# A RetNet and MLP kernel: the first tiles' loads, the late decay tables and the planner's figures

## The chip, the cores and the metric

The kernel runs on one core of a Trainium2 chip. The metric is the device time of one execution in microseconds (us). The engines are PE (matrix products), DVE (vector), ACT (scalar activations), POOL (general purpose) and SP (which here only issues transfers). [...]

## The reference

```python
# q, k, v: (8, 8, 576, 64); x: (4608, 512); w_in: (512, 2048); w_out: (2048, 512); alpha: (2048,)
gamma = 1.0 - 2.0 ** (-5.0 - np.arange(H))
rel = pos[:, None] - pos[None, :]
Dmat = np.where(rel >= 0, gamma[:, None, None] ** rel, 0.0)
ret = (scale * np.matmul(q, k.T) * Dmat) @ v        # per batch and head
x = ret.transpose(0, 2, 1, 3).reshape(B * S, H * D)
h = x @ w_in
out = (np.maximum(h, 0) + alpha * np.minimum(h, 0)) @ w_out
```

First comes a retention layer (attention without softmax, weighted by a decay that falls with distance), then a two-layer MLP whose activation has a slope of its own for each hidden column. All of it is in 32 bit floats.

## The kernel before, in words

**Retention.** A batch has 576 rows, handled in chunks of 64. Within a chunk scores are masked and applied to v; across chunks a state per head is carried on. The decay is put into tables: `tp` holds factors for the rows of q and v, and `gch`, `tabx` and `tabk` hold factors for the carried state, for q and for k of the later pairs. All are computed by small DVE instructions at the head of the program (L117 to L157), before the planned part begins.

The first two batches are done in parts of 256, 256 and 64 rows (`load_part`, `part_scale`, `part_transposes`, `part_scores`, `part_states`, `part_carry`, `part_values`, `last_part`), all eight heads at a time. A part of 256 rows has two tiles each of k, q and v, of 128 rows by 512 columns (256 KB), numbered by `i` (0 is k, 1 is q, 2 is v) and `m`. POOL scales q and v by `tp` (L424); PE turns k and q with transposes (L448), which ACT copies out (L454); PE forms scores (L472), DVE masks them (L478), PE forms states (L494), DVE sums them (L506, L508), and PE forms values (L541, L557), which ACT copies into x (L572). `part_carry` (L514) decays the state for the next part. The other batches are done in pairs of heads (`joint`, with `operands` at L781 and L792), spread over the later work.

**MLP.** Tokens are taken in 18 blocks of 256. The first eight units of the first two blocks are multiplied as plain 32 bit floats (`unit_plain` L1039, `second_plain` L1070). All later ones split x, the weights and the activations into three pieces, and multiply these (`unit` L1108, `unit_two` L1138, `second` L1189). Weights are first converted (`convert`: ACT L670 and L672, DVE L680, L682 and L691, POOL L694) and then split (`split_w`, L723 to L735). The slopes come in as `a16`, 16 rows of 128, and are turned by one PE transpose (L1262) into `malpha` (L1264), which DVE reads for each activation.

**Order.** Nothing of this is issued as written. Each step is recorded by `do(engine, cost, function, reads, writes)`, and `plan()` draws one order: a backward pass gives each step a due time, and a forward pass picks for each engine, from the steps whose inputs would be there, the one that can start earliest, and among those within a small slack the one due first. The planner's clock starts for each engine at `BEGIN`, when the head of the program is taken to be over. A transfer costs 0.56 us of its issuing engine and then occupies one shared wire for its size over a rate; who reads it waits 2.0 us more. Of transfers planned within the first 100 us, an issue by SP also waits, on the chip, for an older one, so that at most 1.25 MiB are in flight (`IN_FLIGHT`, L220 is the line that issues). Steps with `lock` are kept from running beside a locked step of the other one of DVE and POOL.

The costs, the rates and `BEGIN` therefore don't only describe: a change of a figure can change the order of instructions on every engine, and with it which buffer is awaited when.

Of the kernel before, what the change touches and what calls it, by code (L numbers as in the profile page):

```python
# [21 lines left out]
def kernel(  # L22
# [55 lines left out]
    def half(x):  # L78
        return slice(x * C, (x + 1) * C)
# [15 lines left out]
    a16 = const.tile([NFC, P], FP32, name="a16")  # L95
    nc.scalar.dma_start(a16, moe_alpha.rearrange("(t p) -> t p", p=P))
    malpha = const.tile([P, NFC], FP32, name="malpha")
# [44 lines left out]

    nc.vector.reciprocal(pf[:, 1], pf[:, 1])
    nc.vector.tensor_tensor(out=th[:, 1], in0=pf[:, 1], in1=th[:, 2], op=ALU.mult)

    gch = const.tile([P, 3, NPAIR], FP32, name="gch")
    tabx = const.tile([P, NPAIR, 2], FP32, name="tabx")
    tabk = const.tile([P, NPAIR], FP32, name="tabk")
    for h2 in range(2):
        hd = slice(h2 * D, (h2 + 1) * D)  # L150
        nc.vector.tensor_copy(tabk[half(1 - h2)], th[half(1 - h2), 1, h2:H:2])
        nc.vector.tensor_copy(gch[hd, 0], th[hd, 2, h2:H:2])
        nc.vector.tensor_scalar(tabx[hd, :, 0], pf[hd, 0, h2:H:2], QSCALE, None, ALU.mult)
        nc.vector.scalar_tensor_tensor(out=tabx[hd, :, 1], in0=dif[hd, 5, h2:H:2], scalar=1.0,
                                       in1=tabx[hd, :, 0], op0=ALU.add, op1=ALU.mult)
    for i in range(2):
        nc.vector.tensor_tensor(out=gch[:, i + 1], in0=gch[:, i], in1=gch[:, i], op=ALU.mult)  # L157

    for i in range(2):
# [55 lines left out]

    RATE, RATE_256, RATE_128 = 236e3, 175e3, 115e3

# [124 lines left out]
    SLACK, SWITCH = {"PE": 0.3}, {"PE": 0.1}  # L342
    BEGIN = {"PE": 5.0, "ACT": 0.5, "DVE": 8.2, "POOL": 5.8, "SP": 0.5}

# [26 lines left out]
    w32m = [Gen(None) for _ in range(4 * NU)]  # L371
    cst = Gen(None)


# [31 lines left out]

    def load_part(x, which=(0, 1, 2)):
        j0, j1 = PARTS[x % 3]
        for i in which:
            for m in range((j1 - j0 + 1) // 2):  # L410
                s0 = (j0 + 2 * m) * C
                rows = min(P, j1 * C - s0)
                dma(lambda i=i, m=m, rows=rows: part(x, i)[0:rows, m],
                    lambda i=i, s0=s0, rows=rows: (k, q, v)[i][x // 3, :, s0:s0 + rows].rearrange(
                        "h p d -> p h d"), rows * DM * 4, (), [key_p(x, i, m)],
                    "ACT" if x == 0 and i == 1 else "SP", RATE_256)

# [18 lines left out]
    def part_transposes(x, i, bank):  # L436
        t = ((room[x, 3] if i == 0 else Gen((gs[0], op_)[x // 3])) if x % 3 == 0 else
             room[x + i, 3 - 2 * i])

        def at():  # L440
            return words_of(t)[:, 0:1024].rearrange("p (c s) -> p c s", c=NPAIR)
        tT[x, i] = t, at
        for m in range(2):
            pt = Gen(next(bank))

            def f(m=m, pt=pt):
                for c in range(NPAIR):
                    nc.tensor.transpose(pt.get()[:, c * P:(c + 1) * P],  # L448
                                        part(x, i)[:, m, 2 * c:2 * c + 2].rearrange(
                                            "p h d -> p (h d)"), ident)  # L450
            do("PE", 1.0, f, [key_p(x, i, m)], [(pt, 0)])

            def g(m=m, pt=pt):
                nc.scalar.copy(at()[:, :, m * P:(m + 1) * P],  # L454
                               pt.get().rearrange("p (c s) -> p c s", c=NPAIR))
            do("ACT", 0.59, g, [(pt, 0)], [(t, "t", m)])

    def part_scores(x, bank):
        a = Gen((gs[1], ats)[x // 3]) if x % 3 == 0 else room[x + 1, 2]

        def at():
            return words_of(a)[:, 0:1024].rearrange("p (h n) -> p h n", h=2)
        tat[x] = a, at
        (kt, kT), (qt, qT) = tT[x, 0], tT[x, 1]
        ps = [Gen(next(bank)) for _ in range(2)]
        for m in range(2):
            def f(m=m):
                for c in range(NPAIR):
                    for p2 in range(2):
                        for h2 in range(2):  # L470
                            j = chunk(2 * m + p2)
                            nc.tensor.matmul(  # L472
                                ps[h2].get()[half(p2), (2 * c + m) * C:(2 * c + m + 1) * C],
                                kT()[half(h2), c, j], qT()[half(h2), c, j], start=True, stop=True)
            do("PE", 0.9, f, [(kt, "t", m), (qt, "t", m)], [(ps[0], m), (ps[1], m)])
        for h2 in range(2):
            def g(h2=h2):
                nc.vector.tensor_tensor(  # L478
                    out=at()[:, h2].rearrange("p (n s) -> p n s", s=C),
                    in0=ps[h2].get().rearrange("p (n s) -> p n s", s=C),  # L480
                    in1=mask[:, None, :].to_broadcast([P, 8, C]), op=ALU.mult)
            do("DVE", 0.69, g, [(ps[h2], 0), (ps[h2], 1)], [(a, "m", h2)])
# [30 lines left out]
    def part_carry(x):  # L513
        do("POOL", 0.6, lambda: nc.gpsimd.tensor_tensor(  # L514
            out=carry_of(x + 1), in0=sums_of(x, 3),
            in1=gch[:, 2, :, None].to_broadcast([P, NPAIR, D]), op=ALU.mult),
            [sums_key(x, 3)], [carry_key(x + 1)], lock=True)

# [8 lines left out]
    def part_values(x, bank):  # L527
# [7 lines left out]
        for m in range(2):  # L535
            def f(m=m):
                for c in range(NPAIR):
                    for p2 in range(2):
                        for h2 in range(2):
# [5 lines left out]
                                             skip_group_check=True)  # L545
            do("PE", 0.7, f, [key_p(x, 2, m), (a, "m", 0), (a, "m", 1)], [(pv[0], 0), (pv[1], 0)])
        for m in range(2):
            js = [j for j in (2 * m, 2 * m + 1) if j or x % 3]

            def f(js=js):  # L550
                for j in js:
                    su = sums_of(x, j - 1) if j else carry_of(x)
                    for c in range(NPAIR):
                        for h2 in range(2):
                            for e in range(0, D, 32):
# [4 lines left out]
                                                 stop=(j >= 2), skip_group_check=True)  # L560
            do("PE", 0.8, f, [(qt, "t", m)] + [
                sums_key(x, j - 1) if j else carry_key(x) for j in js], [(pv[0], 0), (pv[1], 0)])
# [212 lines left out]
    def operands(n):  # L775
# [3 lines left out]
        def f():  # L779
# [3 lines left out]
                op=ALU.mult)  # L783
        do("POOL", 1.15, f, (), [(qx, a) for a in range(4)], lock=True)
        kT, qT = turned[n] = Gen(kTs[n % 2]), Gen(qTs[n % 2])
# [4 lines left out]
        def f():  # L790
            t = kn.get().rearrange("p j d -> p (j d)")
            nc.scalar.activation(t, t, ACTF.Copy, scale=tabk[:, c:c + 1])  # L792
        do("ACT", 0.78, f, (), [(kn, 0), (kn, 1)])

# [333 lines left out]
    def unit_two(va, vb, u, ga, f):  # L1128
# [3 lines left out]
        def mm():  # L1132
            for p, l in ((p0, 0), (p1, 2), (p0, 1)):
                for cc in range(NCC):
# [4 lines left out]
                                     start=(l != 1 and cc == 0), stop=(l > 0 and cc == NCC - 1))  # L1139
        do("PE", 2.755, mm, x_keys(va, 0) + x_keys(vb, 1) +  # L1140
           [w_at[u, i][l] for i in range(2) for l in range(3)], [(p0, 0), (p1, 0)], kind="pieces")
# [104 lines left out]
    for x in range(3):  # L1246
        rooms(x)
    load_part(0)
    bank = banks_of(0)
# [5 lines left out]
    weights(3)  # L1255
    part_states(0, bank)
    part_carry(0)
    part_values(0, bank)
    weights(1)
    fetch_x(visits[0])  # L1260
    aps = Gen(psa[0])
    do("PE", 0.2, lambda: nc.tensor.transpose(aps.get()[:, 0:NFC], a16, ident[0:NFC, 0:NFC]), (),  # L1262
       [(aps, 0)])
# [263 lines left out]
```

## Time and profile before

| | us |
|---|---|
| three runs, median (lowest to highest) | 943.56 (942.02 to 946.17) |
| the profiled execution, its own time | 940.2 |
| its span, first to last instruction | 938.5 |
| PE busy in the span | 915.6 |
| DVE, ACT, POOL busy | 532.7, 552.9, 578.2 |
| mean granted PE clock | 0.998 of full speed |
| read from HBM, written to it | 74.19 MB, 31.98 MB |

Busy times of different engines lie beside each other and don't add up. A matmul's end is modelled in the profile, so a busy PE is not one at its peak. "L448" is a line of the kernel before; in wait lists the engine or transfer after the arrow is the one that was seen to end last.

### The profile page before, as it was taken

The page shows a single profiled execution, that of the slowest core. Times are in us where ns is not written, and L with a number is a line of the kernel's source. Part 1 is how long each engine was busy: PE and PEld are TensorE (multiplying, and loading weights), DVE is VectorE, ACT ScalarE, POOL GpSimd, SP SyncE. Part 2 cuts the span into 40 slices and gives each one's busy share as a digit, 9 for nine tenths or more (in the row PEclk, how much of TensorE's full clock was granted, in tenths as well). Part 3 has the DMA queues.
Part 4 walks back from the last instruction along what each step waited for, and adds up shares of the span by engine and source line. Part 5 has one row for each costly group of instructions (what it writes and reads, how often), then busy time and mean ns, then how long its engine had stood idle before and what let it go on. Part 6 is the DMA issues. An engine that isn't in the chain of part 4 may idle for free.

```text
span 938.5 us, 21278 instructions
## 1 busy us (share of the span) xinstructions
PE 915.6 (98%) x8241; PEld 777.7 (83%) x8241; DVE 532.7 (57%) x1070; ACT 552.9 (59%) x1175; POOL 578.2 (62%) x491
## 2 busy tenths in 40 slices
PE   5898999999999999999999999999999999999998
PEld 4666688888889898888899988888888888888887
DVE  6668666575766766757664765443444444434333
ACT  4456566657767666665785875645546463635342
POOL 3657775738767577564676465748374656557363
PEclk9999999999999999999999999999999999999999
DMA  9967587788877778886425321121212122221112
GB/s 225 220 186 148 133 199 158 161 177 177 209 175 183 192 180 179 206 188 167 136 90 191 125 90 68 45 90 45 90 45 91 57 90 81 76 80 45 46 45 68
DMA packets 235525, 120.95 MB, mean 129 GB/s; under 512 B 203408, under 2 KB 203424, under 8 KB 235424
## 3 DMA queue, kind: packets, MB, share of 16 engines
q1 hardware_dynamic: 233312, 119.05, 48.3%
q8 instruction: 65, 1.06, 0.5%
q10 hardware_dynamic: 2112, 0.53, 0.3%
q14 instruction: 36, 0.29, 0.1%
HBM read 74.19 MB, written 31.98 MB: 113 GB/s over the span
## 4 chain that ended last, share of the span: by engine, by line
PE 89%; POOL 3%; issue 2%; DVE 1%; ACT 0%; POOLq 0%; ACTq 0%; DVEq 0%
PE pso L1189 40%; PE psh L1108 22%; PE psh L1138 9%; PE psa L1138 9%; PE psh L809 3%; PE psa L870 2%; PE pso L1070 1%; POOL w L424 1%; PE psh L1039 1%; POOL w L733 1%; PE psa L867 1%; PE psh L860 1%; DVE w L735 1%; POOL lx L694 0%; POOL g L694 0%
## 5 line engine op out<-in xcount | busy, mean ns | idle before, releaser
L1189 PE MATMUL pso<-w,g 128*128 128x512 f32 x1416 | 345.1, 391 | 0.0
L1189 PEld LDWEIGHTS pso<-w,g 128*128 128x128 f32 x1416 | 260.1, 188 | 51.0 <-POOL g L1168 0.4
L1108 PE MATMUL psh<-lx,w 128*128 128x256 f32 x1608 | 209.1, 285 | 0.1
L1108 PEld LDWEIGHTS psh<-lx,w 128*128 128x128 f32 x1608 | 202.1, 191 | 7.5 <-issue 0.8
L1168 POOL TENSOR_TENSOR g<-g 128x512 fp32r<-128x512 f32 x136 | 175.8, 1293 | 20.9 <-DVE lx L1014 3.4
L1165 POOL TENSOR_TENSOR g<-ga,g 128x512 fp32r<-128x512 f32 x72 | 93.0, 1292 | 125.7 <-ACT g L1161 94.0
L1116 DVE SCALAR_TENSOR_TENSOR ga<-psh,ga 128x256 f32<-128x256 f32 x144 | 60.6, 421 | 62.6 <-ACT ga L1115 60.4
L1115 ACT COPY ga<-psh 128x256 f32<-128x256 f32 x144 | 53.6, 372 | 70.2 <-PE psh L1108 63.1
L1165 POOL TENSOR_TENSOR g<-x,g 128x512 fp32r<-128x512 f32 x40 | 51.7, 1292 | 62.0 <-ACT g L1161 59.7
L1122 DVE SCALAR_TENSOR_TENSOR ga<-psh,malpha,ga 128x256 f32<-128x256 f32 x144 | 68.6, 477 | 22.5 <-ACT psh L1119 21.8
L1018 POOL TENSOR_TENSOR lx<-lx 128x512 fp32r<-128x512 f32 x48 | 61.8, 1294 | 23.0 <-DVE lx L1014 12.9
L1119 ACT ACTIVATE psh<-ga 128x256 f32<-128x256 f32 x144 | 55.7, 387 | 26.9 <-DVE ga L1116 26.3
L1161 ACT ACTIVATE g<-ga 128x512 fp32r<-128x512 f32 x72 | 45.5, 632 | 24.2 <-DVE ga L1122 14.8
L1165 POOL TENSOR_TENSOR g<-vn,g 128x512 fp32r<-128x512 f32 x24 | 31.0, 1291 | 40.9 <-ACT g L1161 38.3
L888 DVE SCALAR_TENSOR_TENSOR at<-psa,pf,mask 64x512 f32<-64x512 f32 x48 | 36.0, 750 | 33.3 <-PE psa L867 29.1
L1163 ACT ACTIVATE g<-ga 128x512 fp32r<-128x512 f32 x72 | 44.7, 620 | 0.0
L1161 ACT ACTIVATE g<-x 128x512 fp32r<-128x512 f32 x40 | 25.1, 630 | 33.0 <-PE pso L1189 17.2
L1207 DVE TENSOR_TENSOR op<-pso,op 128x512 f32<-128x512 f32 x34 | 23.3, 685 | 36.9 <-PE pso L1189 36.7
L1145 DVE SCALAR_TENSOR_TENSOR x<-psh,x 128x512 f32<-128x512 f32 x20 | 13.8, 689 | 43.9 <-PE psh L1138 42.9
L809 PEld LDWEIGHTS psh<-at,vn 128*64 128x64 f32 x864 | 27.5, 138 | 10.6 <-issue 6.8
L1018 POOL TENSOR_TENSOR w<-w,w 128x256 fp32r<-128x256 f32 x36 | 25.8, 740 | 14.6 <-DVE w L1014 14.6
L1138 PE MATMUL psh<-lx,w 128*128 128x512 f32 x144 | 34.7, 390 | 0.0
(289 smaller groups left out, 1694.0 us busy)
## 6 DMA issues: line engine op xcount, KB each, us to landing
xk<-x SPq DMA_DIRECT2D x18, 512.0 KB, 4.0
out_dram<-o SPq DMA_DIRECT2D x36, 256.0 KB, 2.5
ok<-o SPq DMA_DIRECT2D x34, 256.0 KB, 3.0
x<-xk SPq DMA_DIRECT2D x17, 512.0 KB, 5.5
op<-ok SPq DMA_DIRECT2D x17, 512.0 KB, 3.8
qx<-in_q_dram SPq DMA_DIRECT2D x96, 72.0 KB, 3.2
kx<-in_k_dram SPq DMA_DIRECT2D x96, 72.0 KB, 2.7
kn<-in_k_dram SPq DMA_DIRECT2D x48, 144.0 KB, 3.3
```

The lines of the kernel that those rows point to most:

```text
L809: nc.tensor.matmul(pv[i].get()[half(h2), (j - js[0]) * C:(j - js[0] + 1) * C], vns[n % 2][:, h2, j], mt.get()[:, h2, j], start=True, stop= ...
L1018: lambda l=l, d=d, h=view(0, c): nc.gpsimd.tensor_tensor(out=piece(d()), in0=h(), in1=l(), op=ALU.subtract),
L1108: nc.tensor.matmul(at(b), w[:, c0:c0 + P], xp(l, cc), start=(n == 0 and cc == 0), stop=(n > 0 and cc == NCC - 1), skip_group_check=True)
L1115: do("ACT", 0.36, lambda g=g, at=at: nc.scalar.copy(g(), at(1)), [(ph, 1)], [(ga, f)])
L1116: do("DVE", 0.42, lambda g=g, at=at: nc.vector.scalar_tensor_tensor(out=g(), in0=at(0), scalar=ONE, in1=g(), op0=ALU.mult, op1=ALU.subtrac ...
L1119: do("ACT", 0.39, lambda g=g, at=at: nc.scalar.activation(at(1), g(), ACTF.Relu, scale=-1.0), [(ga, f)], [(ph, 1)])
L1122: do("DVE", 0.48, lambda g=g, at=at, fc=fc: nc.vector.scalar_tensor_tensor(out=g(), in0=at(1), scalar=malpha[:, fc:fc + 1], in1=g(), op0=A ...
L1138: nc.tensor.matmul(p.get(), w[:, c0:c0 + P], piece(words_of(g)[:, o:o + DM]), start=(l != 1 and cc == 0), stop=(l > 0 and cc == NCC - 1))
L1161: do("ACT", 0.64, lambda: nc.scalar.mul(piece(to.get()[:, 2]), whole(), BELOW), both, [(to, 2)])
L1165: do("POOL", 1.29, lambda: nc.gpsimd.tensor_tensor(out=piece(to.get()[:, 1]), in0=whole(), in1=to.get()[:, 2], op=ALU.subtract), both + [( ...
L1168: do("POOL", 1.29, lambda: nc.gpsimd.tensor_tensor(out=piece(to.get()[:, 2]), in0=to.get()[:, 0], in1=to.get()[:, 1], op=ALU.subtract), [( ...
L1189: nc.tensor.matmul(a[2 * m + b].get(), piece(g.get()[:, l, f, m * P:(m + 1) * P]), w_piece(u, 2 + f, l), start=(cell["first"] and f == 0 a ...
```

## The change

The slopes' load leaves ACT's queue at the head and becomes a planned load on SP, just before the transpose that reads it, which now names it as an input. The last part of the decay tables (1/pf, `th[:, 1]`, `tabk`, `gch`, `tabx`) leaves the head and becomes one planned DVE step, `tables`, with the key `(cst, "t")`; the carry, the scaling of q in `operands` and the scaling of k there name this key as an input. The first part's six tiles are all issued by SP, in the order k0, q0, q1, k1, v0, v1; before, both q tiles were issued by ACT and the order on SP was k0, k1, v0, v1. The planner's figures change: two rates, four starts, and the costs of five kinds of PE steps.

```diff
-    nc.scalar.dma_start(a16, moe_alpha.rearrange("(t p) -> t p", p=P))
...
-    nc.vector.reciprocal(pf[:, 1], pf[:, 1])
-    nc.vector.tensor_tensor(out=th[:, 1], in0=pf[:, 1], in1=th[:, 2], op=ALU.mult)
-
...
-    for h2 in range(2):
-        hd = slice(h2 * D, (h2 + 1) * D)
-        nc.vector.tensor_copy(tabk[half(1 - h2)], th[half(1 - h2), 1, h2:H:2])
-        nc.vector.tensor_copy(gch[hd, 0], th[hd, 2, h2:H:2])
...
-    RATE, RATE_256, RATE_128 = 236e3, 175e3, 115e3
+    RATE, RATE_256, RATE_128 = 265e3, 205e3, 115e3
...
-    BEGIN = {"PE": 5.0, "ACT": 0.5, "DVE": 8.2, "POOL": 5.8, "SP": 0.5}
+    BEGIN = {"PE": 3.8, "ACT": 0.5, "DVE": 5.5, "POOL": 5.4, "SP": 0.5}
...
+    def tables():
+        nc.vector.reciprocal(pf[:, 1], pf[:, 1])
+        nc.vector.tensor_tensor(out=th[:, 1], in0=pf[:, 1], in1=th[:, 2], op=ALU.mult)
+        for h2 in range(2):
+            hd = slice(h2 * D, (h2 + 1) * D)
+            nc.vector.tensor_copy(tabk[half(1 - h2)], th[half(1 - h2), 1, h2:H:2])
+            nc.vector.tensor_copy(gch[hd, 0], th[hd, 2, h2:H:2])
+            nc.vector.tensor_scalar(tabx[hd, :, 0], pf[hd, 0, h2:H:2], QSCALE, None, ALU.mult)
+            nc.vector.scalar_tensor_tensor(out=tabx[hd, :, 1], in0=dif[hd, 5, h2:H:2], scalar=1.0,
+                                           in1=tabx[hd, :, 0], op0=ALU.add, op1=ALU.mult)
+        for i in range(2):
+            ins = nc.vector.tensor_tensor(out=gch[:, i + 1], in0=gch[:, i], in1=gch[:, i],
+                                          op=ALU.mult)
+        return ins
...
-    def load_part(x, which=(0, 1, 2)):
+    def load_part(x, which=None):
...
-                    "ACT" if x == 0 and i == 1 else "SP", RATE_256)
+        for i, m in which or [(i, m) for i in range(3) for m in range((j1 - j0 + 1) // 2)]:
...
+                    "h p d -> p h d"), rows * DM * 4, (), [key_p(x, i, m)], rate=RATE_256)
...
-            do("PE", 1.0, f, [key_p(x, i, m)], [(pt, 0)])
+            do("PE", 0.6 if x else 1.0, f, [key_p(x, i, m)], [(pt, 0)])
...
-            do("PE", 0.9, f, [(kt, "t", m), (qt, "t", m)], [(ps[0], m), (ps[1], m)])
+            do("PE", 0.6, f, [(kt, "t", m), (qt, "t", m)], [(ps[0], m), (ps[1], m)])
...
-            [sums_key(x, 3)], [carry_key(x + 1)], lock=True)
+            [sums_key(x, 3), (cst, "t")], [carry_key(x + 1)], lock=True)
...
-            do("PE", 0.7, f, [key_p(x, 2, m), (a, "m", 0), (a, "m", 1)], [(pv[0], 0), (pv[1], 0)])
+            do("PE", 0.6, f, [key_p(x, 2, m), (a, "m", 0), (a, "m", 1)], [(pv[0], 0), (pv[1], 0)])
...
-            do("PE", 0.8, f, [(qt, "t", m)] + [
+            do("PE", 1.0 if len(js) > 1 else 0.6, f, [(qt, "t", m)] + [
...
-        do("POOL", 1.15, f, (), [(qx, a) for a in range(4)], lock=True)
+        do("POOL", 1.15, f, [(cst, "t")], [(qx, a) for a in range(4)], lock=True)
...
-        do("ACT", 0.78, f, (), [(kn, 0), (kn, 1)])
+        do("ACT", 0.78, f, [(cst, "t")], [(kn, 0), (kn, 1)])
...
-        do("PE", 2.755, mm, x_keys(va, 0) + x_keys(vb, 1) +
+        do("PE", 2.73, mm, x_keys(va, 0) + x_keys(vb, 1) +
...
-    load_part(0)
+    load_part(0, ((0, 0), (1, 0), (1, 1), (0, 1), (2, 0), (2, 1)))
...
+    do("DVE", 2.0, tables, (), [(cst, "t")])
     part_carry(0)
...
     fetch_x(visits[0])
+    dma(lambda: a16, lambda: moe_alpha.rearrange("(t p) -> t p", p=P), NFC * P * 4, (), [(cst, "al")])
     aps = Gen(psa[0])
-    do("PE", 0.2, lambda: nc.tensor.transpose(aps.get()[:, 0:NFC], a16, ident[0:NFC, 0:NFC]), (),
+    do("PE", 0.2, lambda: nc.tensor.transpose(aps.get()[:, 0:NFC], a16, ident[0:NFC, 0:NFC]), [(cst, "al")],
```

More of the change, by code (lines that the diff above doesn't have):

```diff
@@ L148 @@
     tabk = const.tile([P, NPAIR], FP32, name="tabk")
-    for h2 in range(2):
-        hd = slice(h2 * D, (h2 + 1) * D)
-        nc.vector.tensor_copy(tabk[half(1 - h2)], th[half(1 - h2), 1, h2:H:2])
-        nc.vector.tensor_copy(gch[hd, 0], th[hd, 2, h2:H:2])
[L153 to L157, printed above, removed]
     for i in range(2):
@@ L405, in carry_key @@
         return room[x, x % 3 + 1], "c"
-    def load_part(x, which=(0, 1, 2)):
+    def load_part(x, which=None):
         j0, j1 = PARTS[x % 3]
[L409 to L415, printed above, removed]
-                    "ACT" if x == 0 and i == 1 else "SP", RATE_256)
+        for i, m in which or [(i, m) for i in range(3) for m in range((j1 - j0 + 1) // 2)]:
+            s0 = (j0 + 2 * m) * C
+            rows = min(P, j1 * C - s0)
+            dma(lambda i=i, m=m, rows=rows: part(x, i)[0:rows, m],
+                lambda i=i, s0=s0, rows=rows: (k, q, v)[i][x // 3, :, s0:s0 + rows].rearrange(
+                    "h p d -> p h d"), rows * DM * 4, (), [key_p(x, i, m)], rate=RATE_256)
     def part_scale(x, i):
```

## The prediction

> **What bounds the kernel now.** I read the page first, then the stretches of ten microseconds, then waits, timeline and DMA issues of the opening. The page says that TensorE (PE) is almost always busy:
>
> ```profile
> span 938.5 us, 21278 instructions
> ...
> PE 915.6 (98%) x8241; PEld 777.7 (83%) x8241; DVE 532.7 (57%) x1070; ACT 552.9 (59%) x1175; POOL 578.2 (62%) x491
> ```
>
> Only 938.5 - 915.6 = 22.9 us are without a matmul. The table of stretches (columns: length, busy time with counts for PE, its weight loads, DVE, ACT and POOL, then clock, DMA share, GB/s) tells where:
>
> ```profile
> 0.00:10.00 10.00, 2.20 (x8) 1.43 (x8) 5.59 (x41) 2.33 (x3) 4.15 (x18) 1.00 0.89 181
> 10.00:20.00 10.00, 8.11 (x297) 7.22 (x297) 5.60 (x10) 4.32 (x9) 3.14 (x3) 1.00 0.99 271
> 20.00:30.00 10.00, 8.32 (x31) 6.16 (x32) 6.38 (x12) 5.00 (x9) 6.59 (x7) 0.83 0.95 268
> ...
> 60.00:70.00 10.00, 10.00 (x252) 7.95 (x252) 7.74 (x14) 5.38 (x12) 6.19 (x6) 1.00 0.34 111
> ```
>
> The first 10 us hold 7.8 us of idle PE, the first 60 hold 14.8; from 60 to 300 there are 3.5, and the end takes 3.7 after the last matmul. From 60 us on the kernel is bound by matmuls that the diff does not touch. So the change can act through the opening, and through the order that the planner draws for everything. The opening, in the timeline (start, duration, engine, line; the bracket is the idle time before and its releaser):
>
> ```profile
> 4.00 1.08 PE L448 MATMUL psa<-ident,w 128*128 128x128 f32 x4 [4.00 <-DMA w<-in_k_dram]
> ...
> 6.97 0.36 DVE L157 TENSOR_TENSOR gch<-gch 128x4 f32<-128x4 f32 x2
> 7.30 1.04 POOL L424 TENSOR_TENSOR w<-w,tp 128x512 f32<-128x512 f32 x1 [4.19 <-DVE gch L157]
> ...
> 8.39 1.11 PE L448 MATMUL pso<-ident,w 128*128 128x128 f32 x4 [3.31 <-POOL w L424]
> 8.94 3.04 POOL L424 TENSOR_TENSOR w<-w,tp 128x512 f32<-128x512 f32 x3 [0.60 <-DMA w<-in_q_dram]
> ...
> 10.04 1.97 PE L448 MATMUL pso<-ident,w 128*128 128x128 f32 x8 [0.53 <-POOL w L424]
> ```
>
> PE turns the first k tile at 4.00, then waits for the scaled q. POOL's wait is put down to DVE L157, but the scale reads only tp, whose last write (L141) ends at 5.48, and POOL starts at 7.30, before L157 ends at 7.33. The DMA issues give the other candidate (last column: us from issue to landing):
>
> ```profile
> w<-in_q_dram ACTq DMA_DIRECT2D x1, 256.0 KB, 5.8
> ```
>
> Issued at 1.29, that tile landed at 7.1. The second q tile (issued 1.88, 6.9 to landing) came at 8.8, which is the wait before 8.94. On SP the k tiles, issued at 0.81 and 1.3, took 3.0 and 4.9: landed 3.8 and 6.2. So q is late because its transfers share the engines with k and v from another queue; the second k tile landed at 6.2 and was turned only after 10.
>
> **What the Trainium skill says.** "DMA: Bandwidth & Descriptors", section "Queues, rings and completion order": each DMA engine takes turns between the queue rows that have work, and within a ring takes descriptors in order. The trace agrees: tiles issued within half a microsecond of each other landed 3.0 us (k, alone at first) and 5.8 us (q, sharing) after issue. "TensorE: Matmul & The Clock Gate", section "What's actually happening": after an idle window of about 3.4 us PE runs at half rate, until about as long a busy one. Here the granted clock was 0.50 from 22 to 24 us after two pauses of 1.61 and 1.38; the 16 matmuls of L1039 took 5.38 us there and 3.72 at 93 us, a loss of 1.66. "SBUF — State Buffer", section "SBUF: two separate sides", states that DVE and GpSimd can hold each other off at one port pair; the trace of before never has a scale of L424 beside the tables, so it shows nothing on that.
>
> **The change part by part.**
>
> *Queue.* Six tiles of 262,144 B go in the order k0, q0, q1, k1, v0, v1. From 2 to 7 us the DMA moved 208, 239, 258, 229 and 218 GB/s, mean 230: one tile each 1.14 us. With k0 at 3.8 as traced: q0 4.9, q1 6.1, k1 7.2, v0 8.4, v1 9.5 (before: 7.1, 8.8, 6.2, 8.3, about 10). SP issues five in some 2.6 us (0.44 to 0.58 each), the sixth waits for k0 by the limit on bytes in flight: 3.8 instead of 7.1. Nothing is late for it.
>
> *POOL.* q0 can be scaled from max(4.9, 5.48 + 0.1) = 5.6 instead of 7.30; tp is now what comes last. One scale is 1.04: q1 from 6.64 instead of 8.94, ready 7.7. Scales of v: 8.5 to 10.6 instead of until 11.98.
>
> *PE.* Transposes of q0 6.75 to 7.85 (1.11), the eight of q1 and k1 until 7.85 + 1.97 = 9.8 instead of 12.01: **-2.2 us**. Scores, masks, states, values follow each other (L472 1.98, L494 1.47, L541 1.55) and move along; v is ready at 10.6, before the states need it at about 11.5.
>
> *Tables.* 1.93 us of DVE (5.40 to 7.33) become one planned step without inputs. DVE has nothing else ready when its planned time begins, so the rule "earliest start first" puts it where it was; cost and gain 0. Its cover is DVE's pause until the first mask (14.05, then about 11.9): 4.5 us. If POOL really waited for DVE, that wait ends at 5.48 too. Port trouble with L424: from 0 to 0.3 (two of the tables' instructions of about 0.16), as q1's scale follows q0's directly; I take 0. The added waits of the carry L514 (22.35), of L781 and of L792 (83.26) come over 10 us after the tables.
>
> *Alpha.* ACT loses its 0.46 us issue and two of 0.59 and 0.77; its table load moves forward, and its first copy waits for PE anyway: 0. SP gets 0.5 us of issue and 8 KB (0.03 us of transfer). The transpose L1262 (0.23) now waits for it; behind it in PE's order stands the first unit (L1039), and before that unit PE had 1.38 us free, waiting for ACT L572. Landing took 4.6 to 5.2 us from issue in that stage: on time if issued before about 14. Bounds: 0 and +5; I take 0.
>
> *Who is late next.* Weights: converted pieces reach DVE L680 at 16.57 and 18.82, while ACT had begun on the raw ones at 12.52 and 14.11, some 4 us of slack less ACT's own 0.7. DMA gains about 0.5 us from its dip at 7 to 9 (156 and 169 GB/s). From 20 to 60 us no compute engine waits for a DMA, and
>
> ```profile
> SPq L220 <- PE psh L557: 3.7, 1, 3.7
> ```
>
> says that a transfer waits for PE there. So the shift should be carried to 60 us and, with PE full, to the end.
>
> *Planner.* New costs are nearer to the trace: four transposes 0.60 (set 1.0, now 0.6), scores 1.16 for both halves (0.9 each, now 0.6), values 1.15 (0.7, now 0.6), L557 1.99 for two (0.8, now 1.0), L1138 2.72 (2.755, now 2.73), transfers 208 to 258 GB/s in 256 B runs (175, now 205). The drawn order changes in ways that no view of before shows. PE's pauses from 16 to 97 us, those against which it could work, are 1.61, 1.38, 0.43, 1.60, 0.23, 0.27, 1.04, 0.20, 0.99 and 1.47, sum 9.2, with 1.66 of low clock. Bounds: half of them gone, -4, to a third more, +3. I take -0.6: truer costs help a little, a redrawn order is a lottery.
>
> Sum: -2.2 + 0 + 0 - 0.6 = **-2.8 us** against the profiled execution's 940.2, so 937.4. The median of the runs shown is 943.56, 3.4 above it; the same shift gives **940.8**.
>
> **Rivals.** (B) The redrawn order also closes pauses: the 1.60 before L1039 at 35.17 (waits for POOL L694) and the low clock's 1.66, with 2.2: -5.5, 938.1. For it: these pauses lie where costs were furthest off. Against: they end in chains of ACT, DVE and POOL whose costs stay. (C) The shift is swallowed: DMA share is 0.95 to 1.08 from 10 to 40 us, so tiles may come no earlier and a wait for a landing takes the pause's place: 0 to -0.7, 943.2. Against: no such wait in 20 to 60 us. (D) Slower: the alpha load stands on SP behind the weights issued from 18.95 to about 21.5 (landing 4.6 to 5.1 later), L1262 is in PE's order ahead of L1039, and PE stands until it lands. Before, L1039 began at 21.26; each microsecond of landing beyond is one lost, and from 26.0 on it is over 4.7 us. Landing at 27 gives +5.7, 949.3. For it: the planner does not know the limit on bytes in flight. Against: it orders by due time, and malpha is needed at 27.3. (E) The tables do not really move, as argued; the rest then decides, and the result is the forecast's.
>
> **How the numbers follow.** About 0.5% (4.7 us) is what a measurement of this kernel can tell from no change. Forecast with E 0.50, 938.5 to 943; B 0.25, mostly below 938.8; C 0.10; D 0.15. So faster 0.25, same 0.60, slower 0.15. The range 936.5 to 946.0 leaves out D and the far end of B.
>
> **What would show it.** Right: L424 first at about 5.6, L472 at about 9.8, first L1039 at about 19, PE in the first 60 us busier by about 2 us, the same 1416 matmuls of L1189 at 391 ns each. Wrong: L424 still at 7, L1039 released by L1262 or by a DMA, or clearly more idle PE after 60 us than the 8.1 us of before.

## The result, and the profile after

| | before | changed | ratio, 95% interval |
|---|---|---|---|
| median, us (ten runs of each) | 941.92 | 937.68 | 0.9945 (0.9926 to 0.9964) |
| lowest to highest | 939.73 to 946.17 | 935.04 to 939.57 | |
| profiled execution, its own time | 940.2 | 939.56 | |
| its span | 938.5 | 937.9 | |

The changed kernel is faster by 4.2 us by the medians and by 5.2 by the ratio. A second series of it (`after_again` below) gave 0.996; weighted by their intervals the two give about 0.9953, or 4.4 us. The forecast said 2.8, rival B 5.5: the truth lies between them. In absolute terms the forecast was 940.8 and the median is 937.68; 1.6 of these 3.1 us are the starting point, since the three runs shown before have a median of 943.56 and the ten of this table 941.92. Three single executions in all, of 1011, 1212 and 1295 us, fell into a slow state and are left out everywhere.

The profiled execution of the changed kernel is one of its slowest: 939.56, where the ten runs reach from 935.04 to 939.57. It shows where instructions moved, but its span must not be taken for the gain. The page:

```profile
span 937.9 us, 21264 instructions
...
PE 915.6 (98%) x8241; PEld 778.5 (83%) x8241; DVE 531.9 (57%) x1070; ACT 552.8 (59%) x1175; POOL 578.8 (62%) x491
```

PE has exactly the work that it had, 915.6 us in 8241 matmuls; all that can differ is its idle time. The opening in the timeline (start, duration, engine, line, operation; in brackets the idle time before it and what ended that). In the changed kernel the DMA issues are L206, the slopes' transpose is L1264 and the tables L362 to L372; the lines from L424 to L1189 kept their numbers.

```profile
4.24 1.09 PE L448 MATMUL psa<-ident,w 128*128 128x128 f32 x4 [4.24 <-DMA w<-in_k_dram]
...
5.41 0.20 DVE L362 RECIPROCAL pf<-pf 128x8 f32<-128x8 f32 x1
...
5.47 1.04 POOL L424 TENSOR_TENSOR w<-w,tp 128x512 f32<-128x512 f32 x1 [2.35 <-DVE tp L139]
5.64 0.90 DVE L363 TENSOR_TENSOR th<-pf,th 128x8 f32<-128x8 f32 x1
6.53 1.57 PEld L448 LDWEIGHTS pso<-ident,w 128*128 128x128 f32 x8 [1.60 <-DMA w<-in_k_dram]
6.53 1.97 PE L448 MATMUL pso<-ident,w 128*128 128x128 f32 x8 [1.20 <-DMA w<-in_k_dram]
...
7.71 1.19 DVE L372 TENSOR_TENSOR gch<-gch 128x4 f32<-128x4 f32 x2
...
7.84 2.17 POOL L424 TENSOR_TENSOR w<-w,tp 128x512 f32<-128x512 f32 x2 [1.33 <-DMA w<-in_q_dram]
...
8.94 1.12 PE L448 MATMUL pso<-ident,w 128*128 128x128 f32 x4 [0.44 <-POOL w L424]
9.98 0.18 PEld L472 LDWEIGHTS pso<-g,w 64*64 64x64 f32 x1 [0.33 <-issue]
```

q0 is scaled at 5.47 instead of 7.30 and q1 at 7.84 instead of 8.94; the scores (L472) begin at 9.98 instead of 11.94. The scores and the first L1039 before, then the first L1039 after:

```profile
11.94 0.36 PE L472 MATMUL pso<-g,w 64*64 64x64 f32 x1
21.26 5.38 PE L1039 MATMUL psh<-x,lx 128*128 128x256 f32 x16 [1.38 <-ACT x L572]
```

```profile
19.15 1.97 PE L1039 MATMUL psh<-x,lx 128*128 128x256 f32 x8 [0.32 <-ACT x L572]
```

The two q tiles in the DMA issues (last column: us from issue to landing), issued by SP at 1.30 and 2.88:

```profile
w<-in_q_dram SPq DMA_DIRECT2D x1, 256.0 KB, 4.0
...
w<-in_q_dram SPq DMA_DIRECT2D x1, 256.0 KB, 4.8
```

They landed at 5.3 and 7.7, where before it was 7.1 and 8.8. The stretches (length, busy time of PE, weight loads, DVE, ACT and POOL, then clock, DMA share, GB/s):

```profile
0.00:10.00 10.00, 4.12 (x19) 3.02 (x19) 7.16 (x41) 3.04 (x4) 5.18 (x18) 1.00 0.97 199
10.00:20.00 10.00, 7.55 (x298) 6.58 (x298) 7.58 (x14) 6.55 (x11) 4.45 (x5) 1.00 1.01 259
20.00:30.00 10.00, 8.61 (x158) 6.45 (x157) 7.81 (x15) 5.80 (x10) 6.38 (x7) 1.00 0.94 260
30.00:40.00 10.00, 5.94 (x200) 4.14 (x199) 7.41 (x12) 3.74 (x7) 8.04 (x8) 0.95 1.07 186
...
60.00:100.00 40.00, 38.70 (x613) 26.62 (x611) 31.35 (x55) 24.56 (x46) 28.79 (x25) 1.00 0.68 149
```

and two of these stretches in the kernel before:

```profile
30.00:40.00 10.00, 8.16 (x154) 6.01 (x153) 6.72 (x12) 5.56 (x10) 4.59 (x4) 1.00 1.08 212
...
60.00:100.00 40.00, 37.54 (x674) 27.15 (x673) 30.11 (x52) 25.30 (x48) 29.89 (x26) 1.00 0.60 130
```

PE gains 1.92 us of work in the first ten. From 60 to 100 it idles 1.3, where the kernel before idles 2.5. But from 30 to 40 its work falls to 5.94, from 8.16 before. PE's waits in the first 60 us, after and then before, show where (total, times, longest):

```profile
PE psa L557 <- issue: 4.1, 1, 4.1
...
PE pso L448 <- POOL w L424: 0.4, 1, 0.4
...
PE psh L1039 <- ACT x L572: 0.3, 1, 0.3
```

```profile
PE pso L448 <- POOL w L424: 3.8, 2, 3.3
PE psh L1039 <- POOL lx L694: 1.8, 2, 1.6
...
PE psh L1039 <- ACT x L572: 1.4, 1, 1.4
PE psh L1039 <- ACT w L596: 1.0, 1, 1.0
```

One pause of 4.06 us inside L557, marked "issue" because the wait list finds no releaser for it (more on it under "Pauses, clock and bytes in flight"), hides most of the gain in this execution; the granted clock is 0.50 from 39 to 42 and the next eight matmuls of L1039 take 3.68 us, against 1.97 for the first eight. The other two lines show what was won: before, PE stood 3.8 us for POOL L424 and 4.2 in all ahead of L1039. Part of this is taken back by waits that are new, 1.2 us for the second k tile and 3.9 in sum for DVE. In all PE idles 14.4 us of the first 60 here, and 14.8 before.

### The profile page after: what moved, and what is told of

Read it like the earlier page. It is cut to its first block, busy times and chain, and to the rows that moved or that the text cites. A ratio compares the mean times of both kernels' runs of the same rounds, so it can differ in the third digit from the quotient of the medians.

```text
span 937.9 us, 21264 instructions
## 1 busy us (share of the span) xinstructions
PE 915.6 (98%) x8241; PEld 778.5 (83%) x8241; DVE 531.9 (57%) x1070; ACT 552.8 (59%) x1175; POOL 578.8 (62%) x491
## 4 chain that ended last, share of the span: by engine, by line
PE 92%; SPq 2%; DMA 2%; issue 1%; DVE 1%; POOL 1%; ACT 1%; POOLq 0%; ACTq 0%; DVEq 0%
PE pso L1189 38%; PE psh L1108 21%; PE psh L1138 9%; PE psa L1138 9%; PE psh L1039 3%; PE pso L1070 3%; PE psh L809 3%; SPq L206 2%; PE psa L870 2%; DMA op<-in_moe_w_out_dram 1%; DMA kn<-in_k_dram 1%; PE psh L860 1%; PE psa L867 1%; DMA w<-in_q_dram 1%; PE psa L472 0%
## 5 line engine op out<-in xcount | busy, mean ns | idle before, releaser
L1189 PE MATMUL pso<-w,g 128*128 128x512 f32 x1416 | 344.7, 391 | 0.0
L1189 PEld LDWEIGHTS pso<-w,g 128*128 128x128 f32 x1416 | 260.2, 188 | 50.6
L1168 POOL TENSOR_TENSOR g<-g 128x512 fp32r<-128x512 f32 x136 | 176.1, 1295 | 23.0 <-DVE w L1014 4.4
L1014 POOL TENSOR_TENSOR lx<-x,lx 128x512 fp32r<-128x512 f32 x24 | 31.0, 1294 | 12.2 <-DVE wa L682 6.2
L809 PE MATMUL psh<-at,vn 128*64 128x64 f32 x864 | 32.7, 226 | 2.5 <-DMA vn<-su 1.3
```

Of the source, the lines that this page charges most:

```text
L809: nc.tensor.matmul(pv[i].get()[half(h2), (j - js[0]) * C:(j - js[0] + 1) * C], vns[n % 2][:, h2, j], mt.get()[:, h2, j], start=True, stop= ...
L1168: do("POOL", 1.29, lambda: nc.gpsimd.tensor_tensor(out=piece(to.get()[:, 2]), in0=to.get()[:, 0], in1=to.get()[:, 1], op=ALU.subtract), [( ...
L1189: nc.tensor.matmul(a[2 * m + b].get(), piece(g.get()[:, l, f, m * P:(m + 1) * P]), w_piece(u, 2 + f, l), start=(cell["first"] and f == 0 a ...
```

## The experiments

A ratio is that to the kernel before on the same chip; its medians there were 941.5, 941.87 and 941.57 in the three groups. It is not the ratio of the medians; where the two tell different sizes, both are given.

### Parts of the change alone

**Queue alone** (`one_queue_old_order`). The order drawn for the kernel before, unchanged; only the six tiles all go by SP, in the order k0, q0, k1, q1, v0, v1 (not the listed one, in which q1 stands ahead of k1).

```diff
-            ins = {"SP": nc.sync, "ACT": nc.scalar}[eng].dma_start(to(), fro())
+            ins = nc.sync.dma_start(to(), fro())
...
+    six = sorted((op for op in drawn if op in first), key=lambda op: RANK[first.index(op)])
+    at6 = [n for n, op in enumerate(drawn) if op in first]
+    for n, op in zip(at6, six):
+        drawn[n] = op
```

> The kernel before with its own drawn order of all steps; only the six tiles of the first part are all issued by SP, in the order k0, q0, k1, q1, v0, v1. Theory 'queue' (q lands earlier, and the shift is carried to the end): first scale of q at about 5.5 instead of 7.3, first scores (L472) at about 10 instead of 11.94, and the time 1.5 to 2.5 us less than before. Rival 'swallowed' (a later wait takes the shift): scores as early, but first L1039 within 0.5 us of 21.26 and the time within 0.5 us of before. Rival 'order alone' (the gain of the change comes from the redrawn order): time as before or up to 1 us less.

Measured: 0.9979 (0.9968 to 0.9991), or -2.0 us; by the medians -1.1. q0 was scaled at 5.50, but the scores came only at 11.16, a miss: q1 landed at about 8.0, and in PE's old order k1 stands behind q1. Nor did the 0.8 us reach the first L1039 in this profile, another miss:

```profile
18.35 1.94 PE L557 MATMUL pso<-g,w 64*32 64x64 f32 x82 [2.17 <-issue]
...
21.64 5.36 PE L1039 MATMUL psh<-x,lx 128*128 128x256 f32 x16 [1.14 <-ACT x L572]
```

The pause before L557 was 1.61 us in the kernel before, and the 82 matmuls behind it took 1.21 there. PE's waits in the first 100 us keep those of the kernel before:

```profile
PE psh L1039 <- POOL lx L694: 1.8, 2, 1.6
PE psh L1039 <- issue: 1.7, 1, 1.7
PE psh L1039 <- ACT x L572: 1.1, 1, 1.1
```

So the queue alone gives a gain, of the size that the forecast gave it by the ratio and of half of it by the medians, though not by the steps it named. The rest of the 4.4 us is elsewhere.

**Figures alone** (`figures_only`): the kernel before with the rates, `BEGIN` and costs of the change, all else as before.

```diff
-    RATE, RATE_256, RATE_128 = 236e3, 175e3, 115e3
+    RATE, RATE_256, RATE_128 = 265e3, 205e3, 115e3
...
-    BEGIN = {"PE": 5.0, "ACT": 0.5, "DVE": 8.2, "POOL": 5.8, "SP": 0.5}
+    BEGIN = {"PE": 3.8, "ACT": 0.5, "DVE": 5.5, "POOL": 5.4, "SP": 0.5}
```

> The kernel before with the new rates, starts and costs of the planner only; q's tiles stay on ACT, tables and slopes in the head. Theory 'queue': q lands at 7.1 as before, first scores at about 11.9, and the time within 1.5 us of before (the redrawn order being worth little). Rival 'order alone': 3 to 5 us less than before, with fewer pauses of PE from 16 to 100 us than the 9.2 us of before.

Measured: 0.9983 (0.9970 to 0.9996), -1.6 us, with q still scaled at 7.26 and the scores at 11.11 (11.9 expected). The figures by themselves do redraw the order for the better, but give less than half.

**All but the figures** (`old_figures`): the changed kernel with the old figures.

```diff
-    RATE, RATE_256, RATE_128 = 265e3, 205e3, 115e3
+    RATE, RATE_256, RATE_128 = 236e3, 175e3, 115e3
...
-    BEGIN = {"PE": 3.8, "ACT": 0.5, "DVE": 5.5, "POOL": 5.4, "SP": 0.5}
+    BEGIN = {"PE": 5.0, "ACT": 0.5, "DVE": 8.2, "POOL": 5.8, "SP": 0.5}
```

> The changed kernel with the old rates, starts and costs. The planner then draws q0 ahead of k0 on SP. Theory 'queue': q0 lands first (about 3.8), so the scale is bound by tp (5.5), k0 comes at about 5; scores at about 10, the time 1.5 to 2.5 us less than before. Rival 'order alone': no gain, within 1 us of before.

Measured: 0.9946 (0.9926 to 0.9967), -5.1 us: the whole gain, without the figures that were meant to be the planner's better knowledge. SP's order came out as q0, k0, q1, k1, v0, v1. Its timeline:

```profile
4.66 1.05 POOL L424 TENSOR_TENSOR w<-w,tp 128x512 f32<-128x512 f32 x1 [1.55 <-DVE th L136]
4.84 0.90 DVE L138 TENSOR_TENSOR tp<-tp,th 128x8 f32<-128x8 f32 x1
```

q0 is scaled at 4.66, while DVE still writes other parts of `tp`: the first scale needs only what L134 wrote by 4.52. The scores began at 9.32 and the first L1039 at 17.48. Waits for POOL ahead of L1039 are still there:

```profile
PE psh L1039 <- POOL w L733: 1.5, 1, 1.5
PE psh L1039 <- POOL lx L694: 1.3, 2, 1.0
```

**q on ACT again** (`q_on_act`): the changed kernel with the old `load_part`, so with the slopes' load gone from ACT's head but q's tiles back on ACT.

```diff
+                    "ACT" if x == 0 and i == 1 else "SP", RATE_256)
...
-    load_part(0, ((0, 0), (1, 0), (1, 1), (0, 1), (2, 0), (2, 1)))
+    load_part(0)
```

> The changed kernel with the queue undone: both q tiles by ACT again, k0, k1, v0, v1 on SP; new figures, planned tables and slopes stay. Theory 'queue': the scale of q waits for its landing until about 7 again, first scores about 12, and the time is 1.5 to 2.5 us above the changed kernel's 937.7 (against the before of the same chip: 2 to 3.5 us less instead of 4 to 5). Rival 'order alone': same as the changed kernel within 1 us.

Measured: 0.9957 (0.9943 to 0.9970), median 937.13, no slower than the changed kernel that can be told; scores at 10.21 instead of the 12 expected. The DMA issues of its ACT queue, the first tile at 0.81:

```profile
w<-in_q_dram ACTq DMA_DIRECT2D x1, 256.0 KB, 4.7
```

With nothing ahead of it q0 landed at 5.5. So it is not the queue's engine that made q late, but what stood before it. The next run isolates that.

**Slopes behind q** (`slopes_last_old_order`): the kernel before, its order, its queues; only the slopes' 8 KB load is issued behind the q tiles.

```diff
-    nc.scalar.dma_start(a16, moe_alpha.rearrange("(t p) -> t p", p=P))
...
+        if op is second_q:
+            nc.scalar.dma_start(a16, moe_alpha.rearrange("(t p) -> t p", p=P))
```

> The kernel before with its own drawn order; only the load of the slopes stands behind the two q tiles on ACT instead of ahead of them. Theory 'ahead in the queue' (the 0.46 us issue of the slopes held q back): q0 is issued at 0.81 instead of 1.29 and lands at about 5.5 instead of 7.1, its scale begins at about 5.6, and the time is 1 to 2 us less than before. The prediction's step (moving the slopes is worth 0): within 0.5 us of before.

Measured: 0.9980 (0.9968 to 0.9991), -1.9 us (-1.6 by the medians): no less than the six tiles on SP by themselves. q0 is scaled at 5.58, and in this profile the shift reaches the first L1039 whole (L423 and L1038 are L424 and L1039 here; 21.26 before):

```profile
5.58 1.04 POOL L423 TENSOR_TENSOR w<-w,tp 128x512 f32<-128x512 f32 x1 [2.47 <-DVE tp L140]
...
19.53 5.38 PE L1038 MATMUL psh<-x,lx 128*128 128x256 f32 x16 [1.38 <-ACT x L571]
```

k0 now comes later: PE's first transposes start at 4.87 instead of 4.00. This part had been put at 0 in the prediction.

**The new order with late q** (`new_order_late_q`): the order drawn for the changed kernel, but the head's loads as before: slopes first on ACT, q tiles behind them there.

```diff
+    nc.scalar.dma_start(a16, moe_alpha.rearrange("(t p) -> t p", p=P))
...
+            eng = "ACT" if on_act and on_act.pop(0) else "SP"
```

> The changed kernel with the order of every step as drawn for it, but with the loads of the head as before: the slopes first on ACT, then both q tiles on ACT, the k and v tiles on SP. With one_queue_old_order it fills a square (old or new order, late or early q). Theory 'queue': q lands at about 7, scores at about 11.5 to 12, and the time is 2 us or more above the changed kernel's (ratio to before 0.997 or more). Rival 'order': the new order brings its gain without the early q, ratio 0.9955 to 0.997. Additive halves would give 0.9945 / 0.9979 = 0.9966.

Measured: 0.9961 (0.9947 to 0.9974), -3.7 us (-3.4 by the medians), with q0 scaled only at 6.78 and the scores at 11.19. PE's waits in the first 100 us hold no wait for POOL L694 any more:

```profile
PE psa L561 <- issue: 2.1, 1, 2.1
PE psh L561 <- issue: 1.9, 1, 1.9
PE psh L1043 <- ACT x L576: 1.0, 1, 1.0
```

(L561, L1043 and L576 are L557, L1039 and L572 here.) The square is complete:

| | q late | q early |
|---|---|---|
| old drawn order | 1 | 0.9979 |
| new drawn order | 0.9961 | 0.9945, again 0.9960 |

The product 0.9979 x 0.9961 = 0.9940 is near the 0.9953 of both together, within the intervals. The order gives the larger part: 3.7 us alone, and 2.4 (0.9979 to 0.9953) where q is early already. The early q gives 2.0 in the old order, but only 0.8 (0.9961 to 0.9953) in the new one, which the intervals do not tell from nothing.

### Which order on SP

**The listed order** (`listed_order`). The planner did not keep the listed order: in the changed kernel SP issues k0, q0, k1, q1, v0, with weights ahead of v1. This run forces the list.

```diff
         last = -min(due)
+        for n, op in enumerate(first):
+            due[op.n] = -last - 100.0 + n
```

> The changed kernel with SP's first loads forced into the order that the change lists: k0, q0, q1, k1, v0, v1, where the planner had drawn k0, q0, k1, q1, v0, two weights, v1. Theory 'landing decides': q1 lands at about 6.5 instead of 7.7, its scale starts at about 6.6, first scores at 9.3 to 9.7 instead of 9.98, first L1039 up to 0.5 us earlier; time 0 to 0.7 us less than the changed kernel. Rival 'redrawn order': the planner draws another order for all the rest, and the time differs by more than 1 us in either direction.

Measured: 0.9962 (0.9944 to 0.9979); scores at 9.64 as expected, the slopes' transpose 0.7 us late, and no time that can be told from the changed kernel's. With the old figures as well (`old_figures_listed`, the two edits together):

> The changed kernel with the planner's old figures and SP's first loads forced to k0, q0, q1, k1, v0, v1. It joins the two cheapest variants. Theory 'landing decides': k0 first lets PE begin at 4.2 instead of 5.5 while q is scaled, scores at about 9.5 (old_figures 9.32): within 0.5 us of old_figures, ratio 0.9945. Theory 'order is a lottery': anywhere from 0.993 to 0.998.

Measured: 0.9944 (0.9928 to 0.9960), median 936.06. Its interval and that of `old_figures` overlap with the changed kernel's 0.9926 to 0.9964, so no version here is shown to beat it.

### Pauses, clock and bytes in flight

**A filled pause** (`filled_pause`): the kernel before with ten needless transposes of the identity in PE's pause before the first L1039.

```diff
+    def slopes():
+        nc.tensor.transpose(aps.get()[:, 0:NFC], a16, ident[0:NFC, 0:NFC])
+        for n in range(10):
+            nc.tensor.transpose(aps.get()[:, P:2 * P], ident, ident)
+    do("PE", 0.2, slopes, (),
```

> The kernel before, with ten more transposes of ident into unused columns behind the slopes' transpose, in the pause of 1.38 us in which PE waits for x; nothing reads them, all else as before. Theory 'clock' (the order before costs 1.7 us because the pauses at 17 and 20 let the clock fall under the first unit): the clock stays at 1.00 from 20 to 25, the first 16 matmuls of L1039 take about 3.7 us instead of 5.4, and the time is 1 to 1.7 us less than before. Rival: the first pause alone lets the clock fall, L1039 stays at 5.4 and the time within 0.5 us of before or up to 0.5 above.

Measured: 0.9995 (0.9983 to 1.0006). Its timeline of PE:

```profile
19.93 1.31 PE L1265 MATMUL psa<-ident 128*128 128x128 f32 x10
21.38 3.69 PE L1039 MATMUL psh<-x,lx 128*128 128x256 f32 x16
...
26.93 2.06 PE L1070 MATMUL pso<-lx,ga 128*128 128x512 f32 x4 [0.98 <-DVE ga L1050]
```

In this profile, with the pause filled, the 16 matmuls take 3.69 us instead of 5.38. But of the 1.7 us only 1.0 is left at L1070 (26.93 for 27.93), where a wait for DVE takes over, and the time of the kernel does not move measurably, a miss against the 1 to 1.7 expected. The interval still allows -1.6 us, and 8 of these 12 executions have a mean clock of 0.998 like the profiled one of the kernel before, so the run alone does not clear the clock.

The clocks of all executions do better. The 132 of the kernel before in the three groups average 941.77 us at a mean clock of 0.9973, the 18 of the changed kernel 937.62 at 0.9982. Among executions of one kernel, 0.001 of clock goes with 0.79 us (one slope fitted within the groups of these 150). By this estimate 0.7 of the 4.2 us between the two averages is clock. At equal clock most of the gain stays: the executions at 0.998 average 941.33 before (58) and 938.08 after (8), those at 1.000 939.45 (22) and 936.85 (4). So rival B's second half, the low clock, is a small part of the gain.

**Fewer and more bytes in flight** (`in_flight_3`, `in_flight_7`): the changed kernel with 768 KiB or 1.75 MiB for the 1.25 MiB. The question was whether the pauses marked "issue" come from instruction fetches held up behind the data of long transfers.

```diff
-    LIMITED, IN_FLIGHT = 100.0, 5 << 18
+    LIMITED, IN_FLIGHT = 100.0, 3 << 18
```

> The changed kernel with at most 768 KiB in flight in the first 100 us instead of 1.25 MiB; the drawn order is the same on every engine. Theory 'instruction fetch behind data' (the unexplained pauses of PE in L557, 4.06 us in the changed kernel's profile, are its instructions coming late behind a long queue of data): the pauses in the first 100 us shrink to under 1.5 us in sum, q1 lands earlier, and the time is 1 to 3 us less. Rival 'a semaphore' (the pause is a wait that the profile doesn't show): pauses as before. Rival 'too few bytes in flight': tiles land later, PE waits for DMA in the first 60 us, time up by 1 us or more.

> The changed kernel with up to 1.75 MiB in flight in the first 100 us instead of 1.25; the drawn order is the same. in_flight_3 was 1.1% slower than the changed kernel by its ratio. Theory 'the bytes in flight bound the opening' goes on: 1 us or more less than the changed kernel. Rival 'saturated at five': within 0.7 us. Rival 'longer queue': q1 and later tiles land later (more than 4.8 us from issue), pauses of PE in L557 grow, 1 us or more above.

Measured: 1.0055 (1.0034 to 1.0076) with 768 KiB, 0.9992 (0.9978 to 1.0006) with 1.75 MiB. The stretch of `in_flight_3` from 10 to 60 us:

```profile
10.00:60.00 50.00, 40.92 (x889) 31.06 (x892) 29.40 (x52) 23.67 (x41) 25.83 (x24) 0.93 0.81 200
```

and the same stretch of the changed kernel:

```profile
10.00:60.00 50.00, 41.50 (x911) 31.52 (x911) 30.61 (x54) 25.98 (x45) 27.23 (x26) 0.97 1.01 239
```

With 768 KiB the engines of the DMA fall from 1.01 busy to 0.81 and from 239 to 200 GB/s. PE's waits of that run in the first 100 us:

```profile
PE psa L448 <- DMA w<-in_k_dram: 6.0, 2, 4.3
PE psa L557 <- issue: 2.7, 1, 2.7
PE psh L557 <- issue: 1.8, 1, 1.8
```

The pauses marked "issue" are there as before (4.5 in sum), now with 1.7 us of waits for a k tile beside the first landing. So nothing supports the second half of the theory, that less data in flight shortens these pauses, and the limit that was set is the best of the three tried.

The first half, that PE waits for its instructions, the kept traces support. Their DMA list has a queue for instructions:

```profile
q8 instruction: 65, 1.06, 0.5%
```

These are 65 packets of 16 KiB, one for 254 of PE's 16,482 matmuls and weight loads. The pauses marked "issue" of three profiles beside them (us; the count is of PE's matmuls and weight loads begun by the end of the pause):

| profile | pause | count | packet moved | PE starts after its landing |
|---|---|---|---|---|
| `before` | 16.90 to 18.51 | 445 | 16.16 to 17.08 | 1.43 |
| `before` | 91.69 to 93.16 | 2978 | 90.71 to 91.81 | 1.35 |
| `after` | 33.96 to 38.02 | 1204 | 35.23 to 36.51 | 1.51 |
| `after` | 89.94 to 91.23 | 2977 | 88.91 to 89.86 | 1.37 |
| `after_again` | 15.76 to 17.23 | 445 | 14.84 to 15.80 | 1.43 |
| `after_again` | 37.46 to 38.50 | 1204 | 35.86 to 37.10 | 1.40 |
| `after_again` | 88.73 to 90.26 | 2977 | 87.54 to 88.82 | 1.44 |

All 33 such pauses of 0.3 us or more in the first 100 us of the 14 profiles end at one of these three counts (within 2), whatever order was drawn, and 1.2 to 1.7 us after a packet has landed. The second and third count lie 759 and 2532 above the first, 3 and 10 times some 253, which is what boundaries between packets would give. In the pause of 4.06 us the packet began to move 1.27 us after PE had run out. What held it back is not shown.

**The changed kernel once more** (`after_again`), no edit, to see whether the pause of 4.06 comes back.

> The changed kernel once more, for a second profile and more runs. If the pause of 4.06 us in L557 and the low clock after it are bad luck of the profiled execution (939.56, the second slowest of its ten): the second profile shows under 3 us of such pauses and a span of 934 to 936. If they belong to the order: a pause of about 4 us at 34 again. Ratio to before 0.9945 plus or minus 0.002 in both cases.

Measured: 0.9960 (0.9942 to 0.9978), median 937.68. Its waits:

```profile
PE psh L557 <- issue: 1.5, 1, 1.5
PE pso L557 <- issue: 1.5, 1, 1.5
PE psa L557 <- issue: 1.0, 1, 1.0
```

The single long pause is gone (1.0 at its place), but the sum is 4.0, a miss against the under 3 expected, and the span is 936.7 (934 to 936 expected). Nor does the first L1039 begin at 19.15 again: here it is 20.95, behind a pause of 1.47 in L557. Over all the profiles of this case the sum in the first 100 us is 3.1 before, 5.4 after, and from 1.0 (`old_figures`) to 5.7 (`in_flight_7`) elsewhere, mostly in L557.

## Why the prediction was right and wrong

**The total came out in range, the split did not.** 937.68 lies in the 936.5 to 946.0 that were given, but below the forecast's own 938.5 to 943, in the band left to rival B. The forecast gave 2.2 us to the queue and 0.6 to the redrawn order; the runs give the order 2.4 to 3.7, and the early q 2.0 alone but only 0.8 within the new order. That the sum came near is in part luck.

**The queue, -2.2: about the right size alone, by partly wrong steps.** q0 landed at 5.3 (predicted 4.9), was scaled at 5.47 (5.6); the scores began at 9.98 (9.8) and the first L1039 at 19.15 (about 19). Measured alone it was -2.0 by the ratio and -1.1 by the medians. The 19.15 is not a firm reading, though: the second profile has 20.95, and with the queue alone it was 21.64. Three steps behind it failed. The order was taken from the list, but the planner drew k1 ahead of q1 (PE turns k1 at 6.53, before q1). SP's issues were put at 0.44 to 0.58 each; after the first two (0.43 and 0.57) they took 0.92, 0.91 and 1.15. Together these brought q1 in at 7.7, not 6.1. And "tp is now what comes last" is wrong: `old_figures` scales at 4.66, before `tp` is complete. It still came out near 9.8 because the forecast let eight transposes follow q1, and in the drawn order only four were left by then: the errors cancelled, which is luck.

**"Alpha: 0": wrong.** The prediction explained q's lateness by sharing with k and v, and counted the slopes' load as 0.46 us of ACT. It cost 1.9 us: it stood 0.48 us ahead of q0 on the same queue, and in `slopes_last_old_order` q0 is scaled 1.7 us earlier for being freed of it. The two gains need not add, since both bring q0's scale to about 5.5; the error in the sum is therefore small. The cause given was not the whole one, but not empty either: with q0 issued at once k0 lands later, so the two queues do share. Why 0.48 us of issue becomes 1.6 us of landing (at 5.5 in `q_on_act`, at 7.1 before) no run settles.

**Tables: 0, as far as the trace shows.** DVE did them at the same place, from 5.41, as rival E had argued; no run moves them alone. The Trainium skill, "SBUF — State Buffer", section "SBUF: two separate sides", had said that DVE and POOL can hold each other off at a shared port. The trace after agrees: L363 took 0.90 us beside the scale of L424 and ended with it (6.54 and 6.51), where its like took 0.17 before, and the two of L372 took 1.19 beside the next scale, where they took 0.36. The prediction took 0 to 0.3 for it, on POOL; 1.6 us fell on DVE instead, and lay inside DVE's pause before the mask.

**Slower by a late load (D): refuted.** SP issued the slopes' load at 10.66 and L1264 ran at 16.36 without a wait. In `old_figures`, `listed_order` and `in_flight_3` it waited 0.9, 0.7 and 0.9 us, not 4.7.

**Swallowed by transfers (C): refuted** for the early q in the old order, by the time of both runs that make only q early (0.9979 and 0.9980) and by the shift at L1038 in one of them. In the new order, where q early brings 0.8 us and no more can be told, it stays open.

**Planner, -0.6: the term that was mis-sized.** The redrawn order is worth 2.4 to 3.7 us by the square above, inside the bounds given (-4 to +3) but four to six times the value taken. The reason given for a small gain, truer costs, does not carry it: the figures alone bring 1.6 us, but with the old figures the rest of the change gains as much as all of it. There, what redraws the order is what is to be ordered: the six loads, the tables and the slopes' load as planned steps. Rival B had the right sign and about the right size, but neither of its mechanisms is shown to earn it. The pauses ahead of L1039 that end at POOL L694 do go away in the changed kernel, but `figures_only` has none of them either and gains 1.6, and `old_figures` keeps 1.3 us of them and gains 5.1. The clock brings some 0.7 by the estimate above.

What within the order earns it is not shown. The weights' conversions come earlier: POOL's eighth L694 starts at 38.10 instead of 44.73 in the changed kernel (41.60 in its second profile), at 40.00 with late q, and at 45.11 with the queue alone, where PE's wait for it stays too. That fits, but `figures_only` converts as early (39.62) and gains only 1.6, so it isn't the whole. Tables and slopes were not moved separately in the new order. The pauses marked "issue" are no part of the answer that could be weighed: they stand at the same three places in PE's instructions in every order, and in two profiles of one kernel the same pause took 4.06 and 1.04 us.

## What to carry to other kernels

Before putting a late transfer down to contention, look at what is issued ahead of it on its own queue: here an 8 KB load that PE first read at 19.65 us cost as much as the choice of queue (1.9 and 2.0 us). A pause without a releaser is worth laying beside the instruction queue's packets and beside the count of instructions. In a planned kernel the order is an edit of its own; to price parts, hold the drawn order fixed and vary the rest, then the reverse, since one run of each corner of that square says what no sum of parts does. And judge effects of half a percent by several runs: the one profile of the changed kernel would have shown 0.6 us, a seventh of the gain.

## What the runs showed of the hardware that was not expected

- PE's clock fell to half after two pauses of 1.61 and 1.38 us (`before`), and of 0.87 and 1.38 (`slopes_last_old_order`), but not after 1.31 and 1.38 (`old_figures_listed`), nor after 1.23 with the second pause filled (`filled_pause`). The Trainium skill, "TensorE: Matmul & The Clock Gate", section "What's actually happening", speaks of an idle window of about 3.4: none of these pauses is that long, and their length alone does not tell when the clock is halved.
- PE stood still, by these signs for its own instructions: pauses of 0.3 to 4.06 us, each at one of three fixed counts of PE's instructions, ended 1.2 to 1.7 us after a 16 KiB packet of the instruction queue had landed.
- Issues of equal tiles by SP took 0.43 and 0.57 us, then 0.92, 0.91 and 1.15.
- A small DVE operation with two inputs (128x8) beside a scale on POOL took 0.90 us instead of 0.17, in `after` (L363) and in `old_figures` (L138).
- DMA throughput from 10 to 60 us rose from 200 to 239 GB/s between 768 KiB and 1.25 MiB in flight; 1.75 MiB (241 GB/s) made the kernel slower again, by 3.6 us (941.26 for 937.68).
